# Eight one-bank PSUM accumulators for the two layers in place of four one-bank tiles and two two-bank tiles

## The chip, the cores and the metric

One NeuronCore of a Trainium2 chip runs the whole program in one launch. The metric is the device time of that launch in microseconds. The kernel before was timed three times (1065.87, 1068.13 and 1069.36 us, median 1068.13), and one more execution was profiled.

## The reference

Block-causal attention for 8 batches and 8 heads (sequence 576, head size 64, blocks of 64), then a normalised two-layer network with a residual. All in float32:

```python
scores = np.matmul(q, k.transpose(0, 1, 3, 2)) / np.sqrt(64)
scores = np.where(block_i >= block_j, scores, -1000000000.0)
attn = softmax(scores)                       # over the last axis
x = np.matmul(attn, v)                       # heads side by side: (8, 576, 512)
xn = (x - mean(x)) / np.sqrt(var(x) + 1e-06) * g_ln
out = x + np.maximum(xn @ w_ch1, 0.0) @ w_ch2   # w_ch1: 512 x 2048, w_ch2: 2048 x 512
```

## The kernel before

**Three stages.** The attention works on 32 pairs of heads. The first layer works on six superblocks of 768 rows and, in each, on eight quads (`quad`, line 762). The second layer works on nine chunks of 512 rows (`second`, line 848). Both layers multiply by a Strassen scheme: seven products instead of eight, numbered 1 to 7, each a float32 product made of three matmuls on a high and a low part per contraction tile. A product is six matmuls on TensorE: 128x384 outputs in the first layer (line 778), 128x256 in the second (line 924).

**PSUM.** PSUM has eight banks, and 512 float32 values per partition fill one. In attention four banks are two score tiles `s` of two banks each (line 272), and the other four are one-bank tiles of the tag `tr` (line 274: transposes, small scores, outputs). The layers need eight accumulators, the list `banks` (lines 757 to 760). `banks[0..3]` are four one-bank tiles `acc` of the tag `tr`. `banks[4]` and `banks[5]` are the two halves of one two-bank tile `y`, which takes a score tile's place, and `banks[6]` and `banks[7]` are the halves of another:

```python
banks = [new_acc() for _ in range(4)]
for _ in range(2):
    two = new_y2()
    banks += [Buf(parent=two, view=lambda t, a=a: t[:, 512 * a:512 * a + 512]) for a in range(2)]
```

**Who uses which bank.** Quad g uses a, b, c = `banks[(3g + k) % 8]`, k = 0, 1, 2 (line 765). Its TensorE order is products 1 (in a), 5 (c), then product 4 of the quad before (in that quad's b), 6 (b), product 3 of the quad before (its c), 2 (a), 7 (b). After product 7 VectorE reads b (line 785, output u3) and then c (c22); then product 4 writes b again and product 3 writes c. ScalarE copies line 787 and line 792 read a.

Chunk n of the second layer gives the seven products, in the order 1, 2, 4, 6, 7, 5, 3 (`ORDER`, line 29), the banks `banks[(7n + k) % 8]`, k = 0..6 (line 862). For contraction steps q = 0 to 5 it goes through all seven products per step. The last two steps, 6 and 7, are run product by product (lines 963, 964), so that each accumulator is complete before the next one's last twelve matmuls. Then VectorE adds accumulators into the result rows `res` (line 941) or into u2 and u4 (lines 948, 949), and ScalarE copies product 1 into p1 (line 945).

**What sets the order.** A planner (`Plan.run`, line 114) walks a simulated timeline and issues each engine's instructions by priority, the TensorE products of both layers as one chain in a fixed order. It tracks readers and writers by `Buf`, so the two halves of a `y` tile are separate for it. The issued order is final. Semaphore waits are then placed by the framework, from which instruction touches which tile. A tile is allocated when its first user is issued; a buffer of the tag `s` also waits until the one allocated before it exists, one of the tag `tr` doesn't (line 267). A `Phase` (line 47) is a pool that opens when the first tile of it is wanted, and not before every instruction that uses the phase before it has been issued; opening closes the phase before.

**Operands.** `prep` (line 668) makes the seven operands of a superblock, each split into a high part (ScalarE cast, line 245) and a low part (VectorE subtraction, line 368; GpSimd does the same for weights), most of them while the last quad of the superblock before runs. In the second layer ha and hb are loaded from DRAM (line 857), and ScalarE and VectorE make the operands hr and hs (lines 882 to 913).

Of the kernel before, what the change touches and what calls it, by code (L numbers as in the profile page):

```python
# [9 lines left out]
F32 = mybir.dt.float32  # L10
# [6 lines left out]
PSUM = bass.MemoryType.PSUM  # L17

P = 128
# [190 lines left out]
def attn_mlp_kernel(ctx: ExitStack, tc: tile.TileContext, qk, qk0, v, v0, w1, w2, g, out):  # L210
# [9 lines left out]
    NPAIR, _, _, S = qk.shape  # L220
# [12 lines left out]
    psum = ctx.enter_context(tc.tile_pool(name="psum", bufs=1, space=PSUM))  # L233
# [16 lines left out]
    attn = Phase(lambda: tc.tile_pool(name="attn", bufs=1))  # L250
    inner = Phase(lambda: tc.tile_pool(name="inner", bufs=1), attn)
    outer = Phase(lambda: tc.tile_pool(name="outer", bufs=1), inner)

    def kind(name, shape, dtype, bufs, space=None, tag=None):

        tag = tag or name
        plan.free.setdefault(tag, bufs)
        phase = space if isinstance(space, Phase) else None

        def make():  # L260
            home = phase.open() if phase else space or sb
            return home.tile(shape, dtype, name=name, tag=tag, bufs=bufs)

        def new():
            x = Buf((tag,), make)
            x.phase = phase
            if tag != "tr":
                x.after, last[tag] = last.get(tag), x
            return x
        return new  # L270

    new_s, new_y2 = (kind(n, [P, 1024], F32, 2, psum, "s") for n in ("s", "y"))
    steps = {}
    new_tr, new_s1, new_o, new_acc = (kind(n, [P, 512], F32, 4, psum, "tr") for n in ("tr", "s1", "o", "acc"))

# [478 lines left out]

    order, hparts = [], {}

    banks = [new_acc() for _ in range(4)]
    for _ in range(2):
        two = new_y2()
        banks += [Buf(parent=two, view=lambda t, a=a: t[:, 512 * a:512 * a + 512]) for a in range(2)]  # L760

    def quad(g, ops):
        sb_, q = divmod(g, 8)
# [208 lines left out]
        order += new  # L972
    plan.chain(order)
    attn.open()
    with tc.manual_schedule(engines={e.engine for e in (nc.tensor, nc.vector, nc.scalar, nc.gpsimd, nc.sync)}):
        plan.run()
    outer.close()


def _run_one(arrays):  # L980
    import numpy as np
    import concourse.bacc as bacc
    from concourse.bass_utils import run_bass_kernel_spmd

    nc = bacc.Bacc("TRN2", target_bir_lowering=False, num_devices=1, dynamic_dma_scratch_size=1024)
    args = {n: nc.dram_tensor(n, a.shape, mybir.dt.from_np(a.dtype), kind="ExternalInput").ap()
            for n, a in arrays.items()}
    for n in ("w1", "w2"):
        args[n] = args[n].bitcast(I32)
    args["out"] = nc.dram_tensor("out_t", (36, P, 512), F32, kind="ExternalOutput").ap()  # L990
    with tile.TileContext(nc) as tc:
        attn_mlp_kernel(tc, *args.values())
    r = run_bass_kernel_spmd(nc, [arrays], core_ids=[0])
    return np.asarray(r.results[0]["out_t"])
# [35 lines left out]
```

## Time and profile before

| | |
|---|---|
| timed, median of 3 | 1068.13 us (1065.87 to 1069.36) |
| the profiled execution's own time | 1069.67 us |
| its span, first to last instruction | 1067.9 us |
| TensorE matmul, busy | 1029.1 us (96%) |
| VectorE, ScalarE, GpSimd, busy | 856.9, 664.8, 278.9 us (80%, 62%, 26%) |
| mean granted TensorE clock | 0.996 |
| attention, first layer, second layer | 0 to 311, 311 to 688, 688 to 1068 us |

Times are in microseconds from the span's start. Engines are PE (TensorE matmul), PEld (its weight loads), DVE (VectorE), ACT (ScalarE), POOL (GpSimd) and SP (the queue that issues DMAs). In a timeline row stand the start, the duration, engine and line, the tiles (out<-in, buffer numbers left out), the shape and the count of instructions merged into the row; in brackets the idle time of the engine before it and what ended it. Tiles `acc` are `banks[0..3]` and tiles `y` are `banks[4..7]`. Matmuls overlap: a row of many is longer than count times the distance of two starts.

### The profile page before, as it was taken

Reading aid. Unit: us, or ns where it says so; the run is one execution under the profiler, and the core shown is the slowest. Engines: PE = TensorE matmul, PEld = TensorE weight load, DVE = VectorE, ACT = ScalarE, POOL = GpSimd, SP = SyncE. Lnnn points to the kernel's source line nnn. Section 1 sums busy time; section 2 is a strip of 40 time slices with the busy share of each in tenths; the row PEclk is TensorE's granted clock in tenths of the full one; section 3 lists DMA queues with packets and bytes.
Section 4 is the critical chain, followed back from the end, with each engine's and each line's share of the span. In section 5 each row is a group of like instructions: output and inputs, shape, how many; then the busy total and the mean of one; then the engine's idle time right before and its main releaser. Section 6 shows DMA issues by size and latency. Waiting matters only on the chain.

```text
span 1067.9 us, 22527 instructions
## 1 busy us (share of the span) xinstructions
PE 1029.1 (96%) x7872; PEld 941.6 (88%) x7872; DVE 856.9 (80%) x1970; ACT 664.8 (62%) x1699; POOL 278.9 (26%) x655
## 2 busy tenths in 40 slices
PE   9999999999989999999999999899999999999997
PEld 6677776777768999999999999899999999999997
DVE  7777799999986696868675488879989798797894
ACT  7988888678883564646341142487757666667650
POOL 4554456333248444243440014300000000000000
PEclk9999999999999999999999999999999999999999
DMA  6655688998756999897975244495765575645731
GB/s 223 193 183 170 180 209 197 219 223 196 175 141 150 244 267 236 256 249 212 253 216 166 101 157 149 155 197 154 166 159 161 119 183 154 159 141 128 185 102 40
DMA packets 375026, 191.29 MB, mean 179 GB/s; under 512 B 235904, under 2 KB 355200, under 8 KB 374912
## 3 DMA queue, kind: packets, MB, share of 16 engines
q1 hardware_dynamic: 374912, 189.85, 67.3%
q8 instruction: 62, 1.02, 0.4%
q14 instruction: 52, 0.43, 0.1%
HBM read 119.54 MB, written 70.25 MB: 178 GB/s over the span
## 4 chain that ended last, share of the span: by engine, by line
PE 79%; DVE 11%; ACT 3%; issue 2%; POOL 2%; DMA 2%; SPq 1%; DVEq 0%; ACTq 0%; POOLq 0%
PE acc L924 16%; PE y L924 16%; PE y L778 15%; PE acc L778 13%; PE s L445 6%; PE tr L472 6%; PE o L482 5%; PE o L478 2%; DVE quad L785 2%; DVE pab L460 1%; DMA raw<-qk 1%; DVE op L368 1%; DVE w L368 1%; ACT pu L463 1%; DVE pu L460 1%
## 5 line engine op out<-in xcount | busy, mean ns | idle before, releaser
L778 PE MATMUL y<-op,w 128*128 128x384 f32 x1008 | 194.0, 339 | 10.9 <-DVE quad L785 10.9
L778 PE MATMUL acc<-op,w 128*128 128x384 f32 x1008 | 190.5, 335 | 4.3 <-DVE op L368 1.6
L778 PEld LDWEIGHTS y<-op,w 128*128 128x128 f32 x1008 | 177.4, 190 | 15.6 <-DVE quad L785 15.2
L778 PEld LDWEIGHTS acc<-op,w 128*128 128x128 f32 x1008 | 175.8, 188 | 6.3 <-DVE op L368 2.4
L924 PE MATMUL y<-w,hs 128*128 128x256 f32 x912 | 120.8, 284 | 7.3 <-DVE u L949 2.3
L924 PEld LDWEIGHTS y<-w,hs 128*128 128x128 f32 x912 | 113.9, 192 | 9.1 <-DVE res L941 3.0
L924 PE MATMUL acc<-w,hs 128*128 128x256 f32 x816 | 107.0, 283 | 0.0
L785 DVE TENSOR_TENSOR quad<-y,quad 128x384 f32<-128x384 f32 x120 | 66.0, 551 | 50.0 <-PE y L778 34.9
L924 PEld LDWEIGHTS acc<-w,hs 128*128 128x128 f32 x816 | 101.9, 192 | 0.0
L445 PE MATMUL s<-raw 64*128 64x320 f32 (+4 forms) x640 | 94.5, 435 | 2.2 <-DMA raw<-qk 1.4
L924 PE MATMUL acc<-w,hr 128*128 128x256 f32 x720 | 95.2, 284 | 0.0
L445 PEld LDWEIGHTS s<-raw 64*128 64x128 f32 x640 | 57.9, 187 | 39.8 <-issue 33.4
L463 ACT ACTIVATE pab<-pab,nm 128x576 f32<-128x576 f32 (+1 forms) x128 | 91.3, 729 | 2.4 <-DVE nm L460 2.4
L785 DVE TENSOR_TENSOR quad<-acc,quad 128x384 f32<-128x384 f32 x120 | 65.9, 551 | 33.6 <-PE acc L778 31.3
L924 PEld LDWEIGHTS acc<-w,hr 128*128 128x128 f32 x720 | 90.9, 193 | 0.0
L460 DVE CUSTOM_DVE_ANT_0 pab<-s,never 128x576 f32<-128x576 f32 (+1 forms) x128 | 82.8, 685 | 3.8 <-PE s L445 3.8
L463 ACT ACTIVATE pu<-pu,nm 128x320 f32<-128x320 f32 (+1 forms) x128 | 64.3, 506 | 33.2 <-DVE nm L460 33.2
L482 PE MATMUL o<-pt,v 128*64 128x256 f32 (+1 forms) x768 | 80.3, 344 | 0.0
L924 PE MATMUL y<-w,hr 128*128 128x256 f32 x576 | 77.0, 284 | 3.0 <-DVE res L941 1.7
L482 PEld LDWEIGHTS o<-pt,v 128*64 128x64 f32 x768 | 56.8, 137 | 26.1
L924 PEld LDWEIGHTS y<-w,hr 128*128 128x128 f32 x576 | 72.4, 192 | 3.8 <-ACT p L945 1.8
L350 POOL TENSOR_SCALAR word<-word 128x512 f32<-128x512 f32 x32 | 49.9, 1560 | 98.6 <-ACT word L348 77.1
(115 smaller groups left out, 1845.2 us busy)
## 6 DMA issues: line engine op xcount, KB each, us to landing
hd<-quad SPq DMA_DIRECT2D x48, 768.0 KB, 4.1
raw<-qk SPq DMA_DIRECT2D x32, 576.0 KB, 5.0
word<-w SPq DMA_DIRECT2D x32, 512.0 KB, 4.7
ha<-hd SPq DMA_DIRECT2D x48, 256.0 KB, 3.3
hb<-hd SPq DMA_DIRECT2D x48, 256.0 KB, 3.0
v<-v SPq DMA_DIRECT2D x32, 320.0 KB, 3.3
x<-xd SPq DMA_DIRECT2D x144, 64.0 KB, 3.5
xw<-xnt SPq DMA_DIRECT2D x144, 64.0 KB, 3.6
```

What stands on the lines that cost most here:

```text
L350: add("POOL", .07 + 512 / 367, lambda: nc.gpsimd.tensor_scalar_max(mag().bitcast(F32), mag().bitcast(F32), 2.0), r=[magn], w=[mag2], prio= ...
L368: add(any_of(lambda e: e.tensor_sub(lo(), src(), hi()), **({} if pool_only else {"DVE": dve(n)}), **({} if fixed else {"POOL": pool(n)})), ...
L445: nc.tensor.matmul(x, raw.t[HALF[h], 0, col], raw.t[HALF[h], 1, at:at + x.shape[1]], start=True, stop=True)
L460: add("DVE", dve(n) + .01, lambda: nc.vector.tensor_tensor_reduce(out=p.t[:, part(i, h)], in0=s.t[:, cols], in1=hide(), scale=-0.125, scal ...
L463: add("ACT", act(n, True) + .14, lambda: nc.scalar.activation(out=p.t[:, part(i, h)], in_=p.t[:, part(i, h)], func=AF.Exp, bias=nm.t[:, at ...
L472: nc.tensor.transpose(o.t[:, n * P:(n + 1) * P], x, ident)
L478: nc.tensor.matmul(o.t[HALF[h], at:at + 256], v_sb.t[:, 0, HALF[h]], z(), start=True, stop=False, skip_group_check=True)
L482: nc.tensor.matmul(o.t[HALF[h], at + lo:at + 256], v_sb.t[:, ck, HALF[h]], rhs(h), start=False, stop=(n == len(steps) - 1), skip_group_che ...
L778: nc.tensor.matmul(where(), w(wi), x(xi), start=start and k == 0 and i == 0, stop=k == 1 and i == 2, skip_group_check=True)
L785: add("DVE", dve(HT) + .09, lambda: nc.vector.tensor_add(slot(o)(), where(), slot(x)()), r=r, w=w, prio=0)
L924: nc.tensor.matmul(acc(name)[:, i], o.t[:, xi, at, P * i:P * i + P], w.t[:, wi, (0, 1, 2, 6, 3, 4, 5)[name - 1]], start=q == 0 and i == 0 ...
```

## The change

The score tiles get a pool of their own, `wide`, which opens before the program. The four accumulators `y` become one-bank tiles in a pool `narrow` that opens in place of `wide`, once every instruction that uses a score tile has been issued; they have no order among themselves. They come first in the list of banks, and the four `acc` tiles come last, so that quad 0 now starts on `y`. The arithmetic, the products' order on TensorE and the formulas that pick a bank are as before.

```diff
+    wide = Phase(lambda: tc.tile_pool(name="wide", bufs=1, space=PSUM))
+    narrow = Phase(lambda: tc.tile_pool(name="narrow", bufs=1, space=PSUM), wide)
...
-            if tag != "tr":
+            if tag not in ("tr", "y"):
                 x.after, last[tag] = last.get(tag), x
...
-    new_s, new_y2 = (kind(n, [P, 1024], F32, 2, psum, "s") for n in ("s", "y"))
+    new_s, new_y = kind("s", [P, 1024], F32, 2, wide), kind("y", [P, 512], F32, 4, narrow)
...
-    banks = [new_acc() for _ in range(4)]
-    for _ in range(2):
-        two = new_y2()
-        banks += [Buf(parent=two, view=lambda t, a=a: t[:, 512 * a:512 * a + 512]) for a in range(2)]
+    banks = [new_y() for _ in range(4)] + [new_acc() for _ in range(4)]
...
     attn.open()
+    wide.open()
...
     outer.close()
+    narrow.close()
```

## Rows read from the trace of the kernel before

**Rows 1.** Windows by stage: us, busy (count) per engine, granted clock, DMA share, GB/s.
```profile
311.00:688.00 377.00, 361.88 (x2049) 354.98 (x2045) 277.02 (x509) 160.56 (x368) 139.62 (x357) 0.99 0.72 202
688.00:1068.00 380.00, 363.73 (x3005) 361.00 (x3003) 313.49 (x659) 246.42 (x616) 0.00 (x0) 1.00 0.59 146
```

**Rows 2.** Costliest groups, second layer: busy, mean ns, idle before and its releaser.
```profile
L924 PE MATMUL y<-w,hs 128*128 128x256 f32 x912 | 120.8, 284 | 7.3 <-DVE u L949 2.3
...
L924 PE MATMUL acc<-w,hs 128*128 128x256 f32 x816 | 107.0, 283 | 0.0
...
L924 PE MATMUL acc<-w,hr 128*128 128x256 f32 x720 | 95.2, 284 | 0.0
...
L924 PE MATMUL y<-w,hr 128*128 128x256 f32 x576 | 77.0, 284 | 3.0 <-DVE res L941 1.7
```

**Rows 3.** TensorE's waits, 688 to 1068 us: total, times, longest; first and last of six.
```profile
PE y L924 <- DVE res L941: 4.0, 5, 0.9
...
PE y L924 <- DVE u L948: 0.9, 1, 0.9
```

**Rows 4.** Timeline of TensorE and VectorE at the end of chunk 1.
```profile
764.29 2.32 PE L924 MATMUL y<-w,hs 128*128 128x256 f32 x18
...
766.65 0.69 DVE L941 TENSOR_TENSOR res<-y,res 128x512 f32<-128x512 f32 x1 [0.70 <-PE y L924]
767.40 0.98 PE L924 MATMUL y<-w,hs 128*128 128x256 f32 x6 [0.78 <-DVE res L941]
...
768.22 1.60 PE L924 MATMUL y<-w,hr 128*128 128x256 f32 x12
```

**Rows 5.** Window of the second layer's chunk 1, columns as in Rows 1.
```profile
724.00:767.00 43.00, 42.02 (x348) 41.81 (x348) 40.88 (x90) 31.03 (x79) 0.00 (x0) 1.00 0.66 165
```

**Rows 6.** TensorE's waits, 345 to 622 us, then 622 to 688 us.
```profile
PE y L778 <- DVE quad L785: 3.8, 7, 1.0
...
PE y L778 <- DVE quad L785: 4.7, 5, 2.9
```

**Rows 7.** Timeline where the second superblock ends: quads 15 and 16.
```profile
435.09 0.56 DVE L785 TENSOR_TENSOR quad<-y,quad 128x384 f32<-128x384 f32 x1 [0.86 <-PE y L778]
...
435.94 2.25 PE L778 MATMUL acc<-op,w 128*128 128x384 f32 x12
...
437.25 0.53 DVE L785 TENSOR_TENSOR quad<-y,quad 128x384 f32<-128x384 f32 x1
...
438.56 0.55 DVE L785 TENSOR_TENSOR quad<-y,quad 128x384 f32<-128x384 f32 x1
439.03 0.95 DVE L368 TENSOR_TENSOR op<-xab,op 128x768 fp32r<-128x768 f32 x1
439.17 1.32 PE L778 MATMUL y<-op,w 128*128 128x384 f32 x6 [0.99 <-DVE quad L785]
```

**Rows 8.** TensorE's timeline: 30 matmuls after a wait, at two places.
```profile
333.23 7.04 PE L778 MATMUL y<-op,w 128*128 128x384 f32 x30 [2.37 <-DVE quad L785]
...
665.06 5.49 PE L778 MATMUL acc<-op,w 128*128 128x384 f32 x30 [1.13 <-DVE quad L785]
```

**Rows 9.** VectorE's timeline, the reads of `y` ahead of that wait's end.
```profile
331.75 0.53 DVE L785 TENSOR_TENSOR quad<-y,quad 128x384 f32<-128x384 f32 x1
...
332.63 0.55 DVE L785 TENSOR_TENSOR quad<-y,quad 128x384 f32<-128x384 f32 x1
```

**Rows 10.** Windows: the stretch behind the first wait of Rows 8, columns as in Rows 1.
```profile
333.20:337.00 3.80, 3.77 (x13) 3.77 (x14) 0.56 (x1) 0.81 (x1) 3.06 (x12) 0.55 0.61 94
```

**Rows 11.** Timeline where attention ends: last score read, operand splits, first products.
```profile
300.67 0.62 DVE L460 CUSTOM_DVE_ANT_0 pab<-s,never 128x448 f32<-128x448 f32 x1
...
309.52 3.99 DVE L368 TENSOR_TENSOR op<-xab,op 128x768 fp32r<-128x768 f32 x2
309.63 3.07 POOL L368 TENSOR_TENSOR w<-word,w 128x1024 fp32r<-128x1024 f32 x1 [0.40 <-ACT w L245]
...
311.85 2.35 PE L778 MATMUL acc<-op,w 128*128 128x384 f32 x12
```

## The prediction

> **What bounds the kernel now.** I read the windows by stage first. In both layers TensorE is busy nearly all the time: 361.9 of 377 us in the first, 363.7 of 380 in the second [rows 1]. Every other engine has room, so a microsecond that TensorE stands still is a microsecond of the result, and nothing else is, as long as its operands come in time. Attention, the first 311 us, touches none of the changed tiles in a new way: the score tiles keep their shape and number.
>
> Next I asked the table of costly groups where TensorE stands still in the second layer. The reader is to see one contrast: groups that write a tile `acc` idle 0.0 us, groups that write a tile `y` idle 7.3 and 3.0 [rows 2]. Same shape, same line, same kind of operands; only the tile differs. The waits of TensorE there come to 10.4 us in 13 waits, in six groups of which the first and last are shown, all of them in front of `y` [rows 3].
>
> The timeline tells what such a wait is [rows 4]. In chunk 1 (n = 1) the seven products have banks 7, 0, 1, 2, 3, 4, 5. The 18 matmuls from 764.29 are product 5 at steps 6 and 7 (bank 4) and product 3 at step 6 (bank 5). Then TensorE waits 0.78 us for the read at 766.65, and goes on with product 3 at step 7, again in bank 5. Nothing reads bank 5 between two steps of one accumulation. What was read is bank 4, the other half of the same two-bank tile. The read itself, 0.70 idle before it, starts only when the 18 matmuls are over, though the last six of them write the half that it doesn't read. So both directions are kept apart by tile, not by bank: the neighbour's read waits for the neighbour's write, and then holds the next write.
>
> **Second layer, counted.** Such a stop comes wherever two products that follow each other in `ORDER` have the banks 4 and 5, or 6 and 7. With bank (7n + k) mod 8 that gives, for n = 0 to 8, 1, 1, 1, 1, 2, 2, 2, 2, 1 stops: 13, as many as the waits [rows 3]. The change gives each accumulator a tile, and all 13 go. Each costs more than its idle time: 18 matmuls take 2.32 us with the last one 0.28 long [rows 2, 4], so one starts every 0.12 us, and the next should have started at 766.45. It started at 767.40, 0.95 late, and its six took 0.82 us to the next start at 768.22 instead of 0.72. That is 1.05 us a stop, 13.65 in all; the bound below is the bare idle time, 10.3.
>
> What is late next? Operands hr and hs, made by VectorE. In chunk 1 VectorE is busy 40.88 of 43 us [rows 5]; without a stop the chunk is some 42. That is the tightest chunk: over the layer it is 313.5 of 380 [rows 1]. I take 0.6 off (0 to 1.05, that chunk's whole gain). Second layer: 13.05.
>
> **First layer.** Here product 4 of a quad writes bank b again after VectorE has read b (u3), and is also held by the read of c (c22) when b and c share a tile: 3g + 1 mod 8 is 4 or 6, so two quads in eight, 12 of 48. One in two of those falls on the last quad of a superblock.
> - Seven waits from 345 to 622 us, 3.8 in all [rows 6]. Followed in the timeline, six of them (3.5 us) end with the neighbour's read and one (0.26) with a read of its own bank. Five are the superblocks' ends (2.95). The pattern at one: u3 is read until 437.78, c22 until 439.11, and product 4 starts at 439.17, 0.99 idle, when it could have gone on at once [rows 7].
> - From 622 to 688 us there are five waits, 4.7 us [rows 6]. Two (1.25) end with the neighbour's read; three, the 2.9 among them, wait for their own bank.
> - The wait of 2.37 us at 333.23 [rows 8]: bank 4's own read ended at 332.28, the neighbour's at 333.18 [rows 9]. 0.90 of it goes, 1.47 stays.
>
> Sum of idle: 3.5 + 1.25 + 0.9 = 5.65. Eight of these waits go whole, and each gives back the same restart loss as above, 1.05 less 0.78, so 8 x 0.27 = 2.2. (Bound below: 0.)
>
> Behind the wait of 2.37 us the granted clock is 0.55 from 333.2 to 337.0, so mostly the lower of the two levels, 1.2 of 2.4 GHz [rows 10], and 30 matmuls take 7.04 us. Behind a wait of 1.13 us 30 take 5.49 [rows 8]. A wait of 1.47 is nearer to the second, so I take the 1.55 as gained (0 to 1.55).
>
> What is late next, here: the operand of product 6, which follows product 4. At the edge of rows 7 its low half is made from 439.03 to 439.98, while TensorE without its wait would want it at about 439.2. But the same false order also holds VectorE: it idles 0.86 before the read at 435.09, of bank 4, waiting for a product in bank 5. VectorE is nearly without a break from there to 439.98, so the split moves up by as much, to 439.12. At edges where VectorE had less idle time, part of the gain turns into a wait for the operand. The five edges together are worth 2.95 + 5 x 0.27 = 4.3; I take 1.0 off (0 to 1.8).
>
> The waits for a read of the own bank stay, and hang on where VectorE is in its queue. They can shrink, since VectorE no longer waits for neighbours (at most their 0.26 + 3.45 + 1.13 = 4.8 in all), or grow, since TensorE comes sooner (I allow 1.0). I take a gain of 0.5. First layer: 5.65 + 2.2 + 1.55 - 1.0 + 0.5 = 8.9.
>
> **The pool and the order of banks.** Quad 0 now takes the banks of the score tiles, and these must be through. The last read of a score tile ends at 301.29, the first product starts at 311.85 [rows 11]: 10.6 us of cover, so the pool's opening costs nothing, and more than that late it costs the excess. The four `acc` tiles are wanted later than now, by quad 1 instead of quad 0. The start is set by VectorE's operand splits, which end at 313.51 [rows 11]; the change makes them neither later nor earlier. No instruction of arithmetic and no DMA is added or taken away.
>
> Sum: 13.05 + 8.9 = 21.95. The profiled execution took 1069.67 us, 1067.9 of it span and 1.8 around it: 1047.7. It lay 1.5 above the median of the timed runs, so by that median it is 1046.2. I predict 1047.
>
> **A rule that speaks against it.** Two operand splits of VectorE took 3.99 us beside a GpSimd subtraction of 3.07 us [rows 11]; one alone takes 0.95 [rows 7], so 2.1 were lost there. If TensorE comes sooner while a split is held like that, the stop only moves from a bank to an operand. The Trainium skill (SBUF — State Buffer, "Who interferes with whom") says that a VectorE instruction with two SBUF inputs contends with a GpSimd one that reads SBUF, and that the second to issue blocks until the first is through; the trace agrees, with the 2.1 us. By that rule the edges could lose all their gain; it is part of the first rival.
>
> **Rivals.**
> - *Operands take the place of the banks.* VectorE's splits, held by GpSimd 2.1 us at each of five edges, would cost 10.5, more than the 8.9 of the first layer, which is then gone. The second layer has no GpSimd work [rows 1] and keeps its 13. Time: 1069.67 - 13 = 1056.7, some 1055 timed. For it: rows 7 and 11. Against: VectorE is itself freed at the edges.
> - *The change doesn't do what it says.* If a wait counted all that VectorE had issued and not what touches the tile, single tiles would wait too: no change, 1068. Against: `acc` idles 0.0 [rows 2], and rows 4 show a wait for which the own bank has no reader at all.
> - *Slower.* The planner runs again with other conditions for its tiles, and may put VectorE's splits for a new superblock behind one more piece of work than now. Then each of the six superblock starts could stop like the worst wait of that layer, 2.9 us [rows 6], with the clock's 1.55 behind it [rows 8]: 6 x 4.45 = 26.7 against the 22 gained, 1074. It decides from 3.7 us a start (22 / 6). Against: the planner already treated the halves as separate, so its order has little reason to move.
>
> **How the numbers follow.** Forecast 0.71, operands 0.20, no change 0.04, slower 0.05. With every bound at its good end the gains are 13.65 + 9.4 + 4.8 = 27.9, so 1041.8; with every bound at its bad end, 10.3 - 1.05 + 5.65 - 1.8 - 1.0 = 12.1, so 1057.6, which takes in the operands' case. The range is 1041 to 1058. About 0.3% (3.2 us) is what a measurement of this kernel can tell from no change. Faster: the first two cases and a little of the planner's, 0.92. Same 0.04, slower 0.04.
>
> **What would show it.** In the second layer TensorE's waits in front of accumulators are down from 13 to none or nearly none, and its window is near 367 us. VectorE's reads of an accumulator start right after its own product. In the first layer the waits at the five superblock ends are gone or are put down to L368 instead of L785, and 30 matmuls near 333 take some 5.5 us. The forecast is wrong if waits of 0.7 to 0.9 us on L941, L948 and L949 are still there, if VectorE's order at the superblock ends differs and TensorE stops there for over 2 us, or if the first product starts much after 312.

## The result and the profile after

The changed kernel takes 1042.65 us in the median of four runs (1041.59 to 1043.19), the kernel before 1067.04 on the same chip (with a fourth run beside the first three): a ratio of 0.9768, with a 95% interval of [0.9747, 0.9788], 24.4 us less. The forecast was 1047 (1041 to 1058). Its profiled execution took 1042.86 us, 26.8 less than the one of before; every step below is read from these two. Of all runs in this document two, which something disturbed, are left out of the times and ratios: one of order_back's four (3609 us) and one of pairs_first's ten (1138 us, at a granted clock of 0.85).

No engine's order of instructions changed. The two traces can be laid on each other matmul by matmul, and the difference in start time grows only where a wait went.

The windows by stage, for the same two stages as in [rows 1]:

```profile
311.00:678.00 367.00, 360.85 (x2064) 358.76 (x2063) 277.31 (x516) 162.66 (x371) 139.38 (x357) 0.99 0.74 209
678.00:1041.00 363.00, 357.27 (x2978) 357.06 (x2976) 309.02 (x652) 243.84 (x612) 0.00 (x0) 1.00 0.61 151
```

TensorE stands still for 6.2 of 367 us in the first layer and 5.7 of 363 in the second, against 15.1 and 16.3 before. The 5.7 are the tail: the last matmul ends at 1035.3 us, and what follows is sums and the output. Up to there, from 678 us on, TensorE has no gap. (These cuts fall on other matmuls than those of before; the table of steps below goes matmul by matmul and has no cuts.) The costliest groups that answer to [rows 2]; the names `y` and `acc` have changed places, because the list of banks now begins with `y`:

```profile
L777 PE MATMUL y<-op,w 128*128 128x384 f32 x1008 | 192.6, 338 | 3.0 <-DVE op L370 1.6
L777 PE MATMUL acc<-op,w 128*128 128x384 f32 x1008 | 190.7, 336 | 3.2 <-DVE quad L784 3.1
...
L923 PE MATMUL acc<-w,hs 128*128 128x256 f32 x912 | 118.6, 283 | 0.0
...
L923 PE MATMUL y<-w,hs 128*128 128x256 f32 x816 | 107.0, 283 | 0.0
...
L923 PE MATMUL y<-w,hr 128*128 128x256 f32 x720 | 95.3, 284 | 0.0
...
L923 PE MATMUL acc<-w,hr 128*128 128x256 f32 x576 | 76.0, 283 | 0.0
```

The 7.3 and 3.0 us of idle time are gone, and no group of the second layer idles. The end of chunk 1, where [rows 4] had the stop, TensorE first and then VectorE:

```profile
747.83 2.32 PE L923 MATMUL y<-w,hs 128*128 128x256 f32 x18
749.99 3.04 PE L923 MATMUL acc<-w,hs 128*128 128x256 f32 x24
```

```profile
748.75 0.69 DVE L947 TENSOR_TENSOR u<-y,p 128x512 f32<-128x512 f32 x1
...
750.19 0.69 DVE L948 TENSOR_TENSOR u<-y,u 128x512 f32<-128x512 f32 x1
...
751.63 1.29 DVE L940 TENSOR_TENSOR res<-acc,res 128x512 f32<-128x512 f32 x2
```

The matmuls go on from one accumulator to the next, and VectorE's reads lie beside them, each in a bank next to one that is being written.

The edge of [rows 7], VectorE and then TensorE:

```profile
433.12 0.55 DVE L784 TENSOR_TENSOR quad<-acc,quad 128x384 f32<-128x384 f32 x1
433.59 0.95 DVE L370 TENSOR_TENSOR op<-xab,op 128x768 fp32r<-128x768 f32 x1
```

```profile
433.62 1.20 PE L777 MATMUL acc<-op,w 128*128 128x384 f32 x6
434.66 1.20 PE L777 MATMUL y<-op,w 128*128 128x384 f32 x6
```

Product 4 starts at 433.62 while c22 is still being read (to 433.67), where it stood 0.99 before. The low half of product 6's operand is done at 434.54, and product 6 starts at 434.66: the operand is 0.12 us ahead.

All waits of TensorE that are left from 311 to 678 us; from 678 on there is none:

```profile
PE acc L777 <- DVE quad L784: 3.1, 2, 2.7
PE y L777 <- DVE op L370: 1.6, 1, 1.6
PE y L777 <- ACT op L245: 1.3, 1, 1.3
```

The last two are the start of the layer and stood before too. The 2.7 at 669 us is a wait for the product's own bank. TensorE and VectorE there:

```profile
669.22 1.53 PE L777 MATMUL acc<-op,w 128*128 128x384 f32 x6 [2.75 <-DVE quad L784]
```

```profile
665.15 0.95 DVE L892 SCALAR_TENSOR_TENSOR sx<-ha,hb 128x256 f32<-128x256 f32 x1
666.03 0.95 DVE L901 TENSOR_TENSOR sy<-hb 128x256 f32<-128x256 f32 x1
666.90 0.94 DVE L892 SCALAR_TENSOR_TENSOR sy<-ha,hb 128x256 f32<-128x256 f32 x1
667.76 0.94 DVE L892 SCALAR_TENSOR_TENSOR sy<-ha,sy 128x256 f32<-128x256 f32 x1
668.63 0.54 DVE L784 TENSOR_TENSOR quad<-acc,quad 128x384 f32<-128x384 f32 x1
```

Sums for the second layer stand ahead of the read in VectorE's queue. These four take 0.95 us each, where the same sums take 0.42 in the median elsewhere in this trace, and GpSimd works beside them (next fence, GpSimd). So the read starts some 2 us later than it could, an estimate from four times the difference:

```profile
664.90 3.52 POOL L837 TENSOR_TENSOR w2f<-w2f 128x256 f32<-128x256 f32 x4
```

### The profile page after: what moved, and what is told of

Read it like the earlier page. It is cut to its first block, busy times and chain, and to the rows that moved or that the text cites. A ratio compares the mean times of both kernels' runs of the same rounds, so it can differ in the third digit from the quotient of the medians.

```text
span 1041.1 us, 22534 instructions
## 1 busy us (share of the span) xinstructions
PE 1022.7 (98%) x7872; PEld 942.2 (91%) x7872; DVE 853.9 (82%) x1970; ACT 664.4 (64%) x1699; POOL 280.0 (27%) x655
## 4 chain that ended last, share of the span: by engine, by line
PE 82%; DVE 8%; ACT 3%; POOL 3%; issue 2%; DMA 2%; SPq 1%; DVEq 0%; ACTq 0%; POOLq 0%
PE y L923 18%; PE acc L923 17%; PE y L777 14%; PE acc L777 13%; PE s L447 6%; PE tr L474 6%; PE o L484 5%; PE o L480 2%; DVE pab L462 1%; ACT pu L465 1%; DVE pu L462 1%; DVE quad L784 1%; ACT pt L245 1%; DVE w L370 1%; DVE pt L247 1%
## 5 line engine op out<-in xcount | busy, mean ns | idle before, releaser
L923 PE MATMUL acc<-w,hs 128*128 128x256 f32 x912 | 118.6, 283 | 0.0
L923 PEld LDWEIGHTS acc<-w,hs 128*128 128x128 f32 x912 | 113.5, 192 | 0.0
L923 PE MATMUL y<-w,hs 128*128 128x256 f32 x816 | 107.0, 283 | 0.0
L923 PEld LDWEIGHTS y<-w,hs 128*128 128x128 f32 x816 | 101.9, 192 | 0.0
L923 PE MATMUL y<-w,hr 128*128 128x256 f32 x720 | 95.3, 284 | 0.0
L923 PEld LDWEIGHTS y<-w,hr 128*128 128x128 f32 x720 | 90.9, 193 | 0.0
L923 PE MATMUL acc<-w,hr 128*128 128x256 f32 x576 | 76.0, 283 | 0.0
L923 PEld LDWEIGHTS acc<-w,hr 128*128 128x128 f32 x576 | 72.1, 192 | 0.0
```

The costliest lines, as they stand in the source:

```text
L923: nc.tensor.matmul(acc(name)[:, i], o.t[:, xi, at, P * i:P * i + P], w.t[:, wi, (0, 1, 2, 6, 3, 4, 5)[name - 1]], start=q == 0 and i == 0 ...
```

## The experiments

Theory: TensorE stood still because a tile of two banks is kept apart as a whole, in two directions: a write of one half waits for the readers of the other, and a read of one half waits for the writers of the other (and for the other engine's read). Rival to it: the gain comes from something else that the edit moved, the pool's place or the order of the banks.

**Both directions put back by hand.** Single tiles in the old order of banks, and for the banks 4 to 7 the waits of the two-bank tiles added one by one, without the two-bank tiles:

```
+     def hold(x, ins, by, *of):        # x: the bank, n ^ 1: its neighbour
+         ...
+         for e in [e for o in of for e in o.get(n ^ 1, {}).values()]:
+             if e.engine != ins.ins.engine:
+                 tc.add_manual_dep(ins.ins, e.name, ...Sync...)
...
+     hold(acc, m, wrote, seen)                  # a matmul waits for the neighbour's readers
+     hold(r[0], nc.vector.tensor_add(...), seen, wrote, seen)   # a read: for its writers and readers
```

> Eight one-bank tiles as after the change, with the list of banks as before (acc first), and by hand the waits of the two-bank tiles put back between the neighbours 4 and 5, 6 and 7: a write waits for the neighbour's reads, a read for the neighbour's writes and for the other engine's reads of it. My theory (the whole gain is these waits, the tiles' shape, the new pool and the order of the list are worth nothing): as slow as the kernel before, 1065 to 1069 us, with 13 stops of 0.7 to 0.9 us in the second layer. Rival (the pool, the order of the list or the tiles' shape carry part): below 1060. If none of it was the waits: 1043.

Measured: 1068.13 us, 1.001 [0.9994, 1.0026] of before. TensorE's waits in the second layer:

```profile
PE y L935 <- DVE res L953: 4.0, 5, 0.9
PE y L935 <- DVE u L961: 2.4, 3, 0.8
PE y L935 <- ACT p L957: 1.4, 2, 0.7
PE y L935 <- ACT hr L898: 0.9, 1, 0.9
PE y L935 <- ACT hr L896: 0.9, 1, 0.9
PE y L935 <- DVE u L960: 0.9, 1, 0.9
```

These are 13 waits and 10.5 us, where [rows 3] belong to 13 and 10.4. The waits alone carry the whole difference; the pool and the tiles' shape carry none that the interval could show.

**One direction at a time.** The same kernel, with the reads free, and with the writes free:

```
- hold(r[0], nc.vector.tensor_add(...), seen, wrote, seen)
+ hold(r[0], nc.vector.tensor_add(...), seen, {})         # write_held: reads wait for nobody
```

```
- hold(acc, m, wrote, seen)
+ hold(acc, m, wrote, {})                                 # read_held: writes wait for nobody
```

> As both_held, but only the writes are held: TensorE waits for the neighbour's reads, the reads are free. My theory: a stop needs both directions. With the reads free, VectorE reads an accumulator some 0.2 us after its own product, beside TensorE's next six matmuls (0.72 us), and has 0.69 us to do; TensorE then stops for 0.2 to 0.3 instead of 0.8. 13 stops of some 0.4 to 0.5 us with the restart are 5 to 6.5 us in the second layer, and in the first some 2 to 5 of the gain stay lost: 1049 to 1054. Rival (the held write alone makes the stops): 1063 to 1068, stops of 0.7 to 0.9 us as before.

> As both_held, but only the reads are held: VectorE and ScalarE wait for the neighbour's writes and for each other, TensorE waits for its own bank alone. My theory: no stop in the second layer, since VectorE's lateness of 0.7 us is hidden there; in the first layer VectorE is later at the five superblock ends and TensorE then waits for operands or for its own bank: 1044 to 1049. Rival (a late read is what costs, the write only follows): 1055 or more.

Measured: with writes held 1055.19 us, 0.9872 [0.9852, 0.9892]; with reads held 1049.26, 0.9822 [0.9804, 0.984]. Against the changed kernel they cost 12.5 and 6.6 us, 19.1 together, and both at once 25.5. The remaining 6.4, of which 4.8 lie in the second layer, belong to the pair: a read that first waits for the neighbour's write ends later, and then holds the neighbour's next write for longer. Both lay just above their expectations. The second layer of write_held (first fence, all waits of TensorE over 0.15 us) shows what a free read leaves: it starts early, but its end still holds the next product, in five places for 0.2 to 0.5 us instead of 0.7 to 0.9, in the others for less, and once, at 717 us, for 1.9. This one stop is the miss: with the granted clock behind it (0.66 from 717 to 722 us) it costs 3.7 of the 8.5 us that the layer lost. The second fence is read_held's first layer, the two costliest groups:

```profile
PE y L935 <- DVE u L961: 1.9, 1, 1.9
PE y L935 <- DVE res L953: 0.9, 2, 0.5
PE y L935 <- DVE u L960: 0.4, 2, 0.3
PE y L935 <- ACT hb L893: 0.2, 1, 0.2
```

```profile
PE y L788 <- DVE quad L796: 3.5, 3, 2.9
PE acc L788 <- DVE op L370: 3.5, 4, 1.6
...
```

Held reads leave the second layer without a wait, and cost in the first: VectorE is late, and with it its splits. Of the four waits for `op` the 1.6 is the start's; the other three come at superblock edges, one of them at 378 us:

```profile
378.31 1.15 PE L788 MATMUL acc<-op,w 128*128 128x384 f32 x5 [0.77 <-DVE op L370]
```

So the operand that the prediction feared does take over at the edges, though only while VectorE itself is held.

One hold on VectorE the prediction didn't count: a read of one half also waits for ScalarE's copy (line 792) of the other half. VectorE's waits in the kernel before, 345 to 688 us:

```profile
DVE quad L785 <- ACT quad L792: 12.7, 9, 2.0
```

In the same stretch both_held has nine such waits (12.5 us) and read_held eight (11.9); write_held and the changed kernel have none.

**The order of the banks.** The changed kernel with the four `acc` tiles first, as before; and the kernel before with its two-bank tiles first, or with their halves four places apart in the list, so that no product follows its neighbour:

```
- banks = [new_y() for _ in range(4)] + [new_acc() for _ in range(4)]
+ banks = [new_acc() for _ in range(4)] + [new_y() for _ in range(4)]          # order_back
```

```
- banks = [new_acc() for _ in range(4)]                                        # pairs_first, tiles of before
+ banks = []
  for _ in range(2):
      ...
+ banks += [new_acc() for _ in range(4)]
+ banks = [single[0], halves[0][0], single[1], halves[1][0],
+          single[2], halves[0][1], single[3], halves[1][1]]                   # apart, tiles of before
```

> After the change, with the list of banks as before: the four acc first, then the four y. My theory: the order is worth nothing, 1041.5 to 1044, with the first product of the first layer where it is after the change, right behind the last of attention. Rival (starting on the score tiles' banks is what lets the first layer begin early): 1046 or more, later from the first product on.

> The kernel before with its two two-bank tiles, only the list of banks turned round: the four halves first, the four acc last, as in the changed kernel. My theory (a stop falls wherever two products that follow each other have the halves of one tile): the halves are now banks 0 and 1, 2 and 3, so the second layer has 2, 2, 2, 2, 1, 1, 1, 1, 2 = 14 stops of 0.7 to 0.9 us in front of y, and the first layer's stops move from the superblocks' last quads to quads 3 and 5 of eight: 1064 to 1070 us. Rival (the order in the list is what the change gained by): near 1043.

> The kernel before with its two two-bank tiles, and a list of banks in which the halves of a tile stand four apart: acc, half, acc, half, acc, other half, acc, other half. My theory: in the second layer no two products that follow each other share a tile, so its 13 stops are gone though the tiles are the old ones: its window is as short as after the change, 12 to 14 us under before. In the first layer product 5 of the next quad now writes the half beside b, one product after product 7, while b is read: up to 24 waits of 0 to 1 us in place of the 9. In all 1046 to 1058. Rival (two-bank tiles are slow in themselves, wherever their halves stand): 1064 or more, with stops in the second layer.

Measured: order_back 1043.46 us (median of three), 0.977 [0.9751, 0.9789]; pairs_first 1068.65 (median of nine), 1.0016 [0.9998, 1.0035], with the 14 waits in the second layer that were expected (11.2 us); apart 1046.59, 0.9799 [0.9767, 0.9832]. Which bank comes first is worth nothing that shows with either kind of tile. What counts is whether the halves follow each other: the old tiles, apart in the list, recover nearly all of the gain. TensorE's waits in apart, 311 to 676 us (a fifth, 0.8 us at 331, is left out); the second layer has none:

```profile
PE y L779 <- DVE quad L786: 3.3, 4, 1.2
PE acc L779 <- DVE quad L786: 2.1, 1, 2.1
PE y L779 <- DVE op L368: 1.6, 1, 1.6
PE y L779 <- ACT op L245: 1.3, 1, 1.3
...
```

It loses to the changed kernel in the first layer: of the four waits in front of a half (3.3 us), three, 2.6 us, end with the read of the other half, because quads that follow each other still bring banks four places apart together.

**One pair.** The changed kernel with the banks 0 and 1 in one tile of two banks, and six single tiles:

```
- banks = [new_y() for _ in range(4)] + [new_acc() for _ in range(4)]
+ two = new_yy()
+ banks = [Buf(parent=two, view=lambda t, a=a: t[:, 512 * a:512 * a + 512]) for a in range(2)]
+ banks += [new_y() for _ in range(2)] + [new_acc() for _ in range(4)]
```

> The changed kernel with banks 0 and 1 again as the halves of one two-bank tile, in the same new pool; the other six are single. My theory (each stop costs its own microsecond, so the loss is in proportion to the stops): banks 0 and 1 follow each other in chunks 0 to 5 and 8, so 7 stops of the second layer come back, 7 x 1.05 = 7.4 us, and in the first layer quad 5 of each eight, up to 6 waits, 0 to 3 us: 1050 to 1053. Rival (a stop that goes alone gains little, since the next one swallows the time): below 1047 or above 1058.

Measured: 1058.72 us, 0.9915 [0.9886, 0.9944]: 16 us lost where 7 to 10 had been expected. By its time alone the rival was met (above 1058), but not for the rival's reason. The second layer (fence below) has seven waits of 5.6 us, 7.3 with their restarts, where the theory gave 7.4: there each stop does cost its own microsecond. The miss lies in the first layer, which took 7.8 us more than in the changed kernel where 0 to 3 had been allowed. Matmul by matmul, 6.5 of these went at seven places: five just behind superblock edges (3.2), and two at 333 and 366 us (1.4 and 1.8). The one at 333 is a wait in front of a single tile: at 320.37 us VectorE's read of one half, whose own product had ended at 318.41, had stood idle for 1.61 us until TensorE's write of the other half was over. Counted from the layer's first matmul VectorE is still some 1.7 us late at 333. The expectation counted the stops of TensorE and not the lateness of VectorE.

```profile
PE yy L926 <- DVE res L943: 2.5, 3, 0.9
PE yy L926 <- ACT p L947: 1.4, 2, 0.7
PE yy L926 <- DVE u L950: 0.9, 1, 0.9
PE yy L926 <- DVE u L951: 0.8, 1, 0.8
```

Two pairs (pairs_first, 26.0 us lost) cost twice as much as one in the second layer, 14.5 against 7.3, but not in the first, 11.1 against 7.8: laid on the changed kernel, pairs_first has the same five losses at the edges as one_pair, and its second pair adds stops elsewhere.

**The wait that is left.** The 2.75 us at 669, taken on by telling the planner what the sums really take beside GpSimd; VectorE's order changes there, and with it ScalarE's in the second layer. Nor is it the order alone, as the expectation has it: the planner also gives three subtractions of weights (`w`), which were VectorE's, to GpSimd. TensorE's order stays:

```
- add("DVE", dve(H), ...)                          # sums sx, sy: L892, L901
+ add("DVE", .95 if n == 0 else dve(H), ...)
```

> The changed kernel, and in the planner the sums of the second layer's chunk 0 on VectorE (lines 892 and 901 of it) are put at 0.95 us, which is what five of them took at 664.7 to 668.7 us beside GpSimd, instead of 0.34. No instruction changes, only the order in which VectorE gets them. My theory of the last wait left (TensorE stops 2.75 us at 669 since VectorE read the accumulator behind these five): the read comes earlier, the wait is gone or under 1 us, with the slow clock behind it: 1037 to 1041. Rival (another queue order only moves the wait): 1041 to 1046.

Measured: 1045.54 us, 0.9794 [0.9762, 0.9825], 2.9 more than the changed kernel, so the theory's time failed and the rival's held. The wait itself went, as the matmuls at 666 to 669 show, but the new order is late with the operands of the last step of chunk 0 (second fence, TensorE at 707 us, with 4.3 us lost by 711):

```profile
666.57 0.87 PE L923 MATMUL y<-w,hr 128*128 128x256 f32 x6
667.38 1.31 PE L777 MATMUL acc<-op,w 128*128 128x384 f32 x6
```

```profile
707.28 0.50 PE L923 MATMUL y<-w,hs 128*128 128x256 f32 x2 [2.22 <-ACT hs L910]
...
710.03 0.51 PE L923 MATMUL acc<-w,hs 128*128 128x256 f32 x2 [0.57 <-ACT hs L910]
```

The operands are converted on ScalarE, whose conversions now stand behind batches of residual scalings (here the batch ahead of the one that ended the 2.22):

```profile
703.86 2.00 ACT L663 ACTIVATE res<-res,sums_all 128x64 f32<-128x64 f32 x8
```

So the time was given back 40 us later. That the same wait could go with the second layer's order left alone was not tried.

## Why the prediction was right, and where its sizes were off

The mechanism was right in its main parts, and the time fell in the range, 4.4 us below the forecast. What was off were sizes, and in one place, at 333 us, the reason. The steps, in us gained between the two profiled executions:

| step | predicted | measured |
|---|---|---|
| 13 stops of the second layer, less chunk 1 | 13.05 | 13.5 |
| five superblock edges | 3.3 | 4.7 |
| wait and slow clock at 333, with the start of the layer | 2.45 | 4.2 - 2.0 = 2.2 |
| other waits for the neighbour | 2.6 | 2.1 to 2.8 |
| waits for the own bank, and remainder | 0.5 | 2.2 to 2.9 |
| attention | 0 | 1.4 |

- **The stops.** All 13 steps between the traces are 0.84 to 1.03 us, with some 0.1 behind each, as worked out (1.05). The 0.6 taken off for chunk 1 was not lost. From 708 to 750 us TensorE has no gap while VectorE is busy 41.62 of 42 us, so [rows 5] showed an engine near its limit. How far it was from costing time, no run shows: the 4.3 us of real_cost went just ahead of that chunk, to ScalarE's conversions.

```profile
708.00:750.00 42.00, 42.00 (x353) 42.00 (x352) 41.62 (x91) 31.98 (x83) 0.00 (x0) 1.00 0.72 182
```

- **The edges.** A term plainly mis-sized: 1.0 was taken off because a split would be late. Nothing was lost; the split moved up with the reads and at the edge shown is still 0.12 us ahead. In the prediction's own words VectorE is "itself freed at the edges", and read_held shows the other case: with VectorE not freed, three of these edges wait for the split.
- **The waits for the own bank.** The term with the largest miss: 0.5 was taken of at most 4.8. At 495.7 us 0.5 went and at 665 us 1.4, because VectorE, no longer held by neighbours, is earlier in its queue: read_held has both waits (0.26 and 1.09 us), write_held neither. Of the wait of 2.9 us [rows 6] 2.75 stayed: the sums that make it don't depend on tiles. This wait and the one behind it, for the neighbour (681 to 686 us of before), gained 1.2 together, which the granted clock behind them mixes; hence the spans in the table.
- **The wait at 333.** The prediction let 0.90 of it go and left 1.47, and took the slow clock behind it as gained. In the changed kernel all of it went, and the 30 matmuls behind it take 5.36 us instead of 7.04 [rows 8]:

```profile
331.26 5.36 PE L777 MATMUL acc<-op,w 128*128 128x384 f32 x30
```

 But TensorE came there 2.0 us late, since its clock had fallen at the start of the layer. VectorE lost nothing there, so it was ahead. Some of this gain is thus a loss that had been taken earlier; the net 2.2 agrees with the forecast for another reason than the one given, which is luck. real_cost, also with single tiles alone, has 0.46 us of the wait back: its clock over 315 to 323 us was 0.79 and not 0.57, so TensorE came earlier, and its product started at 331.42, when its own bank had been read (to 331.36). pairs_first shows this with the old tiles: it lost 4.2 us more than before at the start and had next to no wait at 333, and its time from the layer's start to there and 75 matmuls beyond is the same as that of before within 0.1 us.
- **Attention.** 1.4 us are a wait for a transfer of queries and keys which before had at 190 us and the changed kernel hadn't. In the other profiles that group is between 0 and 1.4 us, whichever tiles they have: chance, not the change. Without it the two profiles differ by 25.4, near the medians' 24.4.
- **The rule on the port.** It cost TensorE nothing at the edges, but makes the wait that is left: the sums there take 0.95 us beside GpSimd and 0.42 elsewhere. The Trainium skill's rule (SBUF — State Buffer, "Who interferes with whom"), that a VectorE instruction with two SBUF inputs contends with a GpSimd one that reads SBUF, agrees with that row.
- **The rivals.** Nothing was reordered, which ends the slower case. Waits are tracked by tile: the changed kernel's own gain, and both_held, end "doesn't do what it says". Operands took over nowhere in the changed kernel; read_held and real_cost show that they are next.

## What to carry to other kernels

Before tuning the order of accumulations, look whether the tiles that hold them span more than one bank: where groups on one-bank tiles idle 0.0 and groups on shared tiles idle, on the same line, the waits are the tile's and not the data's. If the tile must stay, put its halves far apart in the rotation; that alone gave 20.6 us here, where single tiles gave 24.4. And remember that a held read can cost twice, once for the matmul behind it and once for what stands behind it in the reader's queue (in read_held, the splits).

## What the runs showed of the hardware

The granted clock is less steady than [rows 10] made it look. At the start of the first layer all ten profiled kernels have two waits of TensorE of 1.2 to 1.7 us each. Over 315 to 323 us the clock granted behind them was 1.00 in the kernel before and 0.57 in the changed one (fences below, before and after), 0.58 and 0.60 in two others and 0.79 in the remaining six, with either kind of tile:

```profile
315.00:323.00 8.00, 5.68 (x28) 4.83 (x29) 7.90 (x15) 7.40 (x18) 3.22 (x4) 1.00 0.59 175
```

```profile
315.00:323.00 8.00, 6.87 (x24) 6.87 (x25) 6.25 (x13) 5.53 (x15) 4.08 (x11) 0.57 0.42 119
```

Behind the wait at 333 us, on the other hand, both_held kept its clock after 1.66 us where before lost it after 2.37:

```profile
332.62 5.53 PE L788 MATMUL y<-op,w 128*128 128x384 f32 x30 [1.66 <-DVE quad L796]
```

Nor does the length alone decide: real_cost kept its clock after 2.22 us at 707, and write_held lost it after 1.92 us at 717. So a stop of 1.2 to 2.4 us may or may not cost some 2 us more through the clock, and the start of pairs_first, with three stops in a row, lost 4.2. The prediction's choice by "the nearer row" was a guess between two outcomes that both occur. The Trainium skill (TensorE: Matmul & The Clock Gate, "What's actually happening") says that the stretch in which the chip watches TensorE runs freely and isn't reset when the kernel starts, and that the point at which the clock changes varies for that reason. The spread over these runs agrees, but no run shows the mechanism itself. Shorter stops, of 0.7 to 1.0 us, cost no clock in any of the 13 places of the second layer, only 0.2 to 0.3 us at the restart.
